# An attention and two-layer gated network kernel: the last matrix product of batches 2 and 3 in seven 16-bit products

## The chip, the cores and the metric

One core of one Trainium2 chip. The metric is the device time of one execution in microseconds; it is 1033.1 us as the median of 3 runs before the change (1030.32 to 1033.57). PE is TensorE, DVE VectorE, ACT ScalarE, POOL GpSimd, SP the engine whose queue issues the DMAs.

## What is computed

```python
local = softmax(causal(q @ k.T / 8)) @ v                   # 4 batches, 8 heads, 576 x 64
mem   = (phi(q) @ M_prev) / (phi(q) . z_prev + 1e-6)       # phi(x) = elu(x) + 1
x = g * mem + (1 - g) * local                              # (2304, 512) after the heads are joined
x = ((x @ w1) * (x @ w2)) @ w3 @ w_out                     # widths 1024, 1024, 512
y = (sigmoid(x @ w_gate) * (x @ w_val)) @ moe2_w_out       # width 1536, output (2304, 512)
```

All inputs are float32, and all products are made of two parts of each factor, high and low, of which three of the four combinations are added: three matmuls a product of blocks.

## The kernel before

The four batches of 576 tokens run one after the other. Tokens stand as columns, in two halves of 288 (`HS`), features as partitions in blocks of 128. At the start the weights are read as 64-bit bit patterns and turned to float32 (`conv_step`), `w3` and `w_out` are multiplied into one matrix, and the parts of the weights are stored in DRAM, from where they are loaded again for each batch.

Each batch passes through `ffn(b)` in four stages: **ab**, 8 column blocks of `(x@w1)*(x@w2)`; **xw**, 4 blocks of the product with the joined matrix, x2; **gv**, 12 blocks of gate times value, called hg; **ot**, 4 blocks d of the output from the 12 blocks of hg. Attention of the next batch is a generator whose steps `drive` lets in between, in proportion to the costs that `ffn` yields (`FRAC`, `ftot`); in gv none are let in. PE's order is the program's order; on the other engines a scheduler places the instructions.

In batches 0 and 1 all products are plain. In batches 2 and 3, ab and gv are computed by seven products instead of eight (Strassen's scheme in Winograd's form): the two column halves and the two row halves of the operand give x11, x12, x21, x22, sums of these are split into two float16 parts after a scale (`token_steps`, its steps `parts` and `sub`; a split is one ACT and one DVE instruction, `split_scaled`), and the weights have sums of their own. One weight unit of 8 blocks becomes part P (the blocks as they are) and part S (sums of them), each split to 16 bits. This is late work: `late_split` does one step at a time (P, the four sums, S), one step in `pace` calls of `pump`, reads from `kf` and stores to `ka` and `kb`. `two_rows` (line 509) runs the seven products of one column block, each of six matmuls (`prod2`, line 475) in a PSUM bank of its own out of three, and adds on DVE and POOL:

```python
        p1 = product(1, 1, 0, 0)
        s1 = tmp_("cy", "s1")
        nc.scalar.copy(s1, p1)
        p6 = product(6, 0, 0, 2)
        u2 = tmp_("cy", "u2")
        nc.vector.tensor_add(u2, p6, s1)
```

At its end it multiplies gate and value into `hraw` and splits that into two float32r parts, `hg` (`split_rows`, one ACT and one DVE or POOL instruction). The ot stage is plain in all four batches: 4 blocks x 2 halves x 12 blocks of hg x 3 matmuls = 288 (`prod`, line 467), an ACT copy to `osb` and one store for each block.

`pump` also loads weights ahead (`load_step`, line 382): five slots, in the last batch eight. `tails` (line 789) puts the steps that prepare x of batches 2 and 3 into `pending`, whose items run one by one among the ot products before.

## Time and profile before

| | |
|---|---|
| time, median of 3 runs | 1033.1 us |
| the profiled execution | 1028.78 us |
| its span, first to last instruction | 1026.8 us |
| mean granted TensorE clock | 0.993 |
| busy DVE, ACT, POOL | 684.5, 571.8, 247.4 us |
| DMA | 224.83 MB, mean 219 GB/s |

In the trace the stages begin at about these times: batch 0's gv at 263, ot at 345; batch 1's ab 385, xw 471, gv 504, ot 574; batch 2's ab 629, xw 698, gv 734, ot 796; batch 3's ab 855, xw 899, gv 923, ot 985. A wait is read from the bracket at the end of a timeline row: the idle time of the engine before it and what ended it. A product and its weight load are two rows, PE and PEld, and overlap. The granted clock is given as a share of 2.4 GHz. A group's mean is that of single instructions; where instructions run on, the timeline merges them, and their common length over their count is the time in which one gives way to the next.

### The profile page before, as it was taken

What the parts mean: (1) busy time and instruction counts of PE and PEld (TensorE: products, weight loads), DVE (VectorE), ACT (ScalarE), POOL (GpSimd) and SP (SyncE); (2) the same over time, 40 slices, a digit from 0 to 9 for tenths busy, and PEclk for the clock granted to TensorE, in tenths of its full rate; (3) what the DMA queues carried; (4) which work ended last, traced back from release to release, by engine and by line L of the source; (5) the groups of instructions that cost most, each with busy time, mean ns of one, the idle gap of its engine ahead of it and who ended that gap; (6) DMA issues with size and microseconds to landing.
All of it is one profiled execution on the core that took longest, in us unless ns stands there. A gap on an engine that the chain in (4) does not pass through costs nothing.

```text
span 1026.8 us, 19856 instructions
## 1 busy us (share of the span) xinstructions
PE 1000.1 (97%) x7382; PEld 834.0 (81%) x7382; DVE 684.5 (67%) x1596; ACT 571.8 (56%) x1179; POOL 247.4 (24%) x246
## 2 busy tenths in 40 slices
PE   7999999999999998999999999899999999999998
PEld 3556787888999898898977788677877888897798
DVE  6865888778776627765566659998877427837730
ACT  7977786567777635654455444455644433235420
POOL 3454021212000201321101012453244302403420
PEclk9989999999999999999999999999999999999999
DMA  8865799857776479863777588655755335545551
GB/s 294 249 214 197 260 345 314 307 193 262 243 248 223 159 252 372 293 201 99 266 245 243 207 282 311 187 182 162 226 179 187 112 112 190 196 150 162 186 193 56
DMA packets 80376, 224.83 MB, mean 219 GB/s; under 512 B 10520, under 2 KB 22936, under 8 KB 80280
## 3 DMA queue, kind: packets, MB, share of 16 engines
q1 hardware_dynamic: 80280, 223.57, 64.2%
q8 instruction: 58, 0.95, 0.4%
q14 instruction: 38, 0.31, 0.1%
HBM read 165.34 MB, written 58.20 MB: 218 GB/s over the span
## 4 chain that ended last, share of the span: by engine, by line
PE 76%; DVE 6%; ACT 2%; issue 1%; DMA 1%; POOL 0%; SPq 0%; DVEq 0%; ACTq 0%; POOLq 0%
PE gv L467 14%; PE ot L467 14%; PE gvp L478 12%; PE ab L467 9%; PE xw L467 9%; PE abp L478 6%; PE s L902 3%; PE t L963 3%; PE o L1031 3%; PE o L1016 1%; PE wps L467 1%; PE o L1024 1%; DMA wraw<-kf 1%; DVE p L907 1%; PE qt L1000 0%
## 5 line engine op out<-in xcount | busy, mean ns | idle before, releaser
L478 PEld LDWEIGHTS <-wslot 128*128 128x128 f16 x1680 | 163.0, 98 | 47.3 <-issue 5.9
L933 POOL TENSOR_SCALAR p<-p,sm,omg 116x116 f32<-116x116 f32 (+4 forms) x100 | 87.3, 877 | 325.4 <-DVE sm L931 187.2
L467 PE MATMUL ot<-hg,wslot 128*128 128x288 f32 x1152 | 165.7, 299 | 0.0
L467 PEld LDWEIGHTS ot<-hg,wslot 128*128 128x128 f32 x1152 | 154.5, 188 | 6.5 <-issue 5.5
L467 PE MATMUL gv<-x,wslot 128*128 128x288 f32 (+1 forms) x1152 | 147.5, 290 | 0.2 <-ACT gsb L134 0.2
L478 PE MATMUL gvp<-x,wslot 128*128 128x288 f16 x1008 | 124.3, 286 | 1.1 <-DVE x L177 1.1
L467 PE MATMUL ab<-x,wslot 128*128 128x288 f32 x768 | 121.0, 308 | 0.2 <-DVE wpart L597 0.2
L134 ACT ACTIVATE p<-p,sm 116x116 f32<-116x116 f32 (+4 forms) x160 | 92.9, 583 | 43.7 <-DVE sm L907 43.5
L467 PE MATMUL xw<-h,wslot 128*128 128x288 f32 x768 | 113.7, 300 | 2.4 <-ACT h L570 1.1
L467 PEld LDWEIGHTS ab<-x,wslot 128*128 128x128 f32 x768 | 107.2, 193 | 7.9 <-issue 5.0
L467 PEld LDWEIGHTS xw<-h,wslot 128*128 128x128 f32 x768 | 103.6, 188 | 7.4 <-issue 3.0
L907 DVE CUSTOM_DVE_ANT_0 p<-s,msk 116x116 f32<-116x116 f32 (+4 forms) x160 | 67.9, 454 | 36.1 <-PE s L902 35.5
L478 PE MATMUL abp<-x,wslot 128*128 128x288 f16 x672 | 87.4, 286 | 1.7 <-DVE c11ab L544 1.2
L572 DVE TENSOR_TENSOR wslot<-wraw,wslot 128x512 fp32r<-128x512 f32 x76 | 56.1, 740 | 40.3 <-ACT wslot L570 40.0
L467 PEld LDWEIGHTS gv<-x,wslot 128*128 128x128 f32 x576 | 76.4, 188 | 0.5 <-ACT gsb L134 0.5
L963 PE MATMUL t<-idf,p 116*116 116x116 f32 x480 | 67.6, 270 | 6.4 <-DVE p L933 3.9
L963 PEld LDWEIGHTS t<-idf,p 116*116 116x116 f32 x480 | 53.6, 137 | 20.7 <-issue 5.2
L467 PEld LDWEIGHTS <-wslot 128*128 128x128 f16 x576 | 56.3, 98 | 14.2
L353 ACT ACTIVATE cy<-r 128x512 f32<-128x512 f32 x76 | 51.3, 675 | 12.0 <-DVE wraw L362 2.4
L570 ACT CAST wslot<-wraw 128x512 fp32r<-128x512 f32 x76 | 47.0, 620 | 17.3 <-PE gv L467 7.4
L362 DVE SCALAR_TENSOR_TENSOR wraw<-cy,cr 128x512 int32<-128x512 int32 x76 | 54.0, 738 | 2.5 <-ACT cr L354 2.3
L981 ACT COPY pt<-t 116x696 f32<-116x696 f32 (+2 forms) x74 | 47.2, 647 | 9.5 <-PE t L963 9.2
(156 smaller groups left out, 1550.5 us busy)
## 6 DMA issues: line engine op xcount, KB each, us to landing
wslot<-k SPq DMA_DIRECT2D x76, 512.0 KB, 4.2
wslot<-ka SPq DMA_DIRECT2D x40, 512.0 KB, 4.0
k<-wslot SPq DMA_DIRECT2D x36, 512.0 KB, 3.7
wraw<-kf SPq DMA_DIRECT2D x32, 512.0 KB, 6.6
wslot<-kb SPq DMA_DIRECT2D x40, 384.0 KB, 3.9
r<-in_gv_dram SPq DMA_DIRECT2D x24, 512.0 KB, 5.2
kf<-wraw SPq DMA_DIRECT2D x20, 512.0 KB, 3.2
ka<-wS SPq DMA_DIRECT2D x20, 512.0 KB, 4.9
```

Source lines behind the costliest of these rows:

```text
L134: ins = nc.scalar.activation(**kw)
L353: nc.scalar.activation(out=y, in_=hi, func=AF.Prelu, scale=2.0**-112, alpha=2.0**32)
L362: nc.vector.scalar_tensor_tensor(z, y, 3, tmp["r"], ALU.logical_shift_left, ALU.bitwise_or)
L467: paced["pe"] = nc.tensor.matmul(ps, w[:, wi, blk, :], x[:, xi, cols : cols + n], start=first and part == 0, stop=last and part == 2,)
L478: paced["pe"] = nc.tensor.matmul(ps, w[:, wi, blk + k, :], x[:, xi, k, :], start=k == 0 and part == 0, stop=k == 1 and part == 2,)
L570: nc.scalar.copy(dst[:, 0], src)
L572: eng.tensor_sub(dst[:, 1], src, dst[:, 0].bitcast(F32))
L902: nc.tensor.matmul(os_[hh], q_[r, 0, i * T : (i + 1) * T], k_[r, 1, c0:c1], start=x == 0, stop=x == len(terms) - 1,)
L907: nc.vector.tensor_tensor_reduce(out=ps_[hh][:, c0:c1], in0=os_[hh], in1=msk[:, SP - w + c0 : SP - w + c1], scale=-0.125, scalar=3.0e38 if ...
L933: lower(SHARE_N).tensor_scalar(ps_[hh][:, :w], ps_[hh][:, :w], sm[:, 6 + hh : 7 + hh], omg[:T, 2 * p + hh : 2 * p + hh + 1], ALU.mult, ALU ...
L963: nc.tensor.transpose(tp[:T, c : c + T], src[hh][:, j * T : (j + 1) * T], idf[:T, :T])
L981: nc.scalar.copy(to, got)
```

## The change

The ot stage of batches 2 and 3 is computed by seven 16-bit products too (`out_rows`, new). The 12 blocks of hg are four blocks each in three groups g; each group is quartered and turned into seven operands by `token_steps`. For a pair of output blocks (dp, two of them) each product is a sum over the three groups: 18 matmuls. The first three products open the three PSUM banks; three others are added onto these banks after they have been read; the seventh has a bank of its own. The order on PE is products 0, 1, 2 on group 0, then on group 1, then on group 2, and then products 3 to 6, each over its three groups.

With it come
- six more late weight tasks for `o2` (P and S each, from `ko` into `op` and `os`, stored in pieces), between those of gv and of ab, and a scale for them (`o2_scale`), from maxima taken in batch 0;
- in gv of batches 2 and 3: the blocks are left whole as `hq`, four to a group, in the buffers of the late work; a group's steps go into `queue`, and `two_rows` takes two of them a column block (`flush(1)`); the rest run before `out_rows`. A scale of hg (`hg_scale`) comes from maxima of x2;
- `two_rows`: products 2, 7 and 3 are added onto the banks of products 1, 6 and 5 after these are read; one DVE and one POOL addition fewer, in ab one ACT copy more;
- x of batches 2 and 3: the three sums that need no scale are made ahead of it (`tails`);
- five weight slots in the last batch too; output stores by halves; `FRAC` by batch (0.89 in batch 2), other paces.

```diff
-PACE = (5, 4, 4, 14, 4)
+PACE = (4, 4, 3, 14, 8, 4)
...
+    tasks = [(u, "P") for u in jobs[:F2]] + [(("o", *x), "PS") for x in pairs_of]
+    NFIRST = len(tasks)
+    tasks += [(u, "PS") for u in jobs[F2:]]
+    NPARTS = len(tasks)
+    tasks += [(u, "S") for u in jobs[:F2]]
...
     def two_rows(...):
-        p2 = product(2, 1, 2, 5)
+        product(2, 1, 2, 5, a)
         c11 = tmp_("asb", "c11")
-        nc.vector.tensor_add(c11, p2, s1)
-        gate(c11)
-        p7 = product(7, 0, 6, 3)
+        if sigmoid:
+            act_fn(out=c11, in_=a, func=AF.Sigmoid, scale=by)
+        else:
+            nc.scalar.copy(c11, a)
+        product(7, 0, 6, 3, b)
         u3 = tmp_("cr", "u3")
-        nc.vector.tensor_add(u3, p7, u2)
-        p3 = product(3, 0, 2, 4)
+        nc.vector.tensor_add(u3, b, s1)
+        product(3, 0, 2, 4, c)
...
+    def out_rows(b, dp, x, by):
+        s = take(7)
+        banks = {}
+        def product(i, g, xo):
+            onto = {3: 0, 4: 2, 5: 1}.get(i, i)
+            if onto == i and g == 0:
+                banks[i] = ps_f.tile([128, 512], F32, tag="f", name=f"otp{b}_{dp}_{i}")[:, :HS]
+            w = slot(s + i)
+            for k in range(2):
+                for part, (wi, xi) in enumerate(((0, 0), (1, 0), (0, 1))):
+                    paced["pe"] = nc.tensor.matmul(
+                        banks[onto], w[:, wi, 2 * g + k, :], x[g][xo][:, xi, k, :],
...
+        for g in range(2):
+            for i, xo in ((0, 0), (1, 1), (2, 2)):
+                product(i, g, xo)
+        p1 = product(0, 2, 0)
+        nc.scalar.activation(out=s1, in_=p1, func=AF.Copy, scale=by[:, 0:1])
+        p5 = product(1, 2, 1)
+        nc.scalar.activation(out=s5, in_=p5, func=AF.Copy, scale=by[:, 0:1])
+        p6 = product(2, 2, 2)
+        plus(u2, p6, s1)
+        for i, xo in ((3, 5), (4, 3), (5, 4), (6, 6)):
+            for g in range(3):
+                ps = product(i, g, xo)
...
     gv of batches 2 and 3:
+                for _ in two_rows(take(2), x2, f"gv{b}_{f}", left, right, x2back[:, f : f + 1], True):
+                    pass
+                if f == 2:
+                    hgs, oback = hg_scale(b, x2top, x2s)
+                if f % 4 == 3:
+                    steps = token_steps(f"hg{b}_{g}", *quads, hg, lambda: hgs[:, 0:1], tags, tied=True)
+                    first = [steps[x] for x in ("p0", "t1", "p1", "t2", "p2")]
+                    then = [steps[x] for x in ("p5", "t3", "p3", "p4", "t4", "p6")]
+                    if g == 2:
+                        n = max(0, len(queue) - len(then))
+                        rest = [None] * (len(then) - len(queue[n:])) + queue[n:]
+                        queue[n:] = first
+                        for a, z in ((0, 1), (1, 3), (3, 4), (4, 6)):
+                            queue.extend(x for x in rest[a:z] + then[a:z] if x)
+                    else:
+                        queue.extend(first + then)
...
+        flush(len(queue))
+        for dp in range(2 if b > 1 else 0):
+            yield from out_rows(b, dp, hs, oback)
```

**DVE, end of batch 3's gv.** The names: `gvp_11` is the last block's products, `hraw` and `hq` its result, `hg` the split operands; `hq_8_0`, `hq_8_1`, `hq_10_0`, `hq_10_1` are the four quarters of the third group, and `hg_2_0`, `hg_2_2`, `hg_2_5`, `hg_2_6` hold its operands 0 and 1, 2 and 3, 5 and 4, 6. Before:

```order
L534 TENSOR_TENSOR u2gv_11_12487<-gvp_11_6_12480,s1gv_11_12478 128x288
L572 TENSOR_TENSOR hg_10_12391<-hgraw_10_12392,hg_10_12391 128x576
L544 TENSOR_TENSOR c11gv_11_12507<-gvp_11_2_12500,s1gv_11_12478 128x288
L549 TENSOR_TENSOR u3gv_11_12517<-gvp_11_7_12510,u2gv_11_12487 128x288
L553 TENSOR_TENSOR u4gv_11_12498<-gvp_11_3_12519,u4gv_11_12498 128x288
L559 TENSOR_TENSOR u3gv_11_12517<-u3gv_11_12517,gvp_11_4_12529 128x288
L525 SCALAR_TENSOR_TENSOR hgraw_11_12468<-s5gv_11_12496,x2back_11441,u4gv_11_12498 128x288
L525 SCALAR_TENSOR_TENSOR hgraw_11_12468<-u3gv_11_12517,x2back_11441,c11gv_11_12507 128x288
```

Here the last block ends DVE's work ahead of the output. After the change, from the last block's two multiplications on (three more steps of the second group stand between the last subtraction and these):

```order
L585 SCALAR_TENSOR_TENSOR hq_10_1_12395<-s5gv_11_12493,x2back_11494,u2gv_11_12483 128x288
L585 SCALAR_TENSOR_TENSOR hq_10_0_12394<-u3gv_11_12512,x2back_11494,c11gv_11_12504 128x288
L181 SCALAR_TENSOR_TENSOR hg_2_0_12535<-hq_8_0_12251,hgs_11890,hg_2_0_12535 128x576
L555 TENSOR_TENSOR hq_8_1_12252<-hq_10_1_12395,hq_8_1_12252 128x576
L181 SCALAR_TENSOR_TENSOR hg_1_6_12562<-hq_6_0_12108,hgs_11890,hg_1_6_12562 128x576
L181 SCALAR_TENSOR_TENSOR hg_2_5_12548<-hq_10_1_12395,hgs_11890,hg_2_5_12548 128x576
L555 TENSOR_TENSOR hq_8_0_12251<-hq_10_1_12395,hq_8_0_12251 128x576
L181 SCALAR_TENSOR_TENSOR hg_2_5_12548<-hq_10_0_12394,hgs_11890,hg_2_5_12548 128x576
L181 SCALAR_TENSOR_TENSOR hg_2_2_12542<-hq_8_1_12252,hgs_11890,hg_2_2_12542 128x576
L555 TENSOR_TENSOR hq_10_0_12394<-hq_8_0_12251,hq_10_0_12394 128x576
L181 SCALAR_TENSOR_TENSOR hg_2_2_12542<-hq_8_0_12251,hgs_11890,hg_2_2_12542 128x576
L181 SCALAR_TENSOR_TENSOR hg_2_6_12566<-hq_10_0_12394,hgs_11890,hg_2_6_12566 128x576
```

The row that writes `hg_2_2` from `hq_8_0` is operand 2, which product 2 on the third group reads; it stands eleventh here, behind operands 4, 5 and 3 of its group and operand 6 of the group before.

**ACT, the same place.** Before, the last gate, the cast of the last block, and the output copies:

```order
L134 ACTIVATE c11gv_11_12507<-c11gv_11_12507,x2back_11441 128x288
L134 ACTIVATE u4gv_11_12498<-u4gv_11_12498,x2back_11441 128x288
L570 CAST hg_11_12467<-hgraw_11_12468 128x576
L758 COPY osb_0_12543<-ot_0_0_12544 128x288
L758 COPY osb_0_12543<-ot_0_1_12584 128x288
```

After, the high parts of the operands, with the readings of the first two output products (`s1ot`, `s5ot`) between them:

```order
L180 ACTIVATE hg_2_0_12535<-hq_8_0_12251,hgs_11890 128x576
L180 ACTIVATE hg_1_6_12562<-hq_6_0_12108,hgs_11890 128x576
L180 ACTIVATE hg_2_5_12548<-hq_10_1_12395,hgs_11890 128x576
L180 ACTIVATE hg_2_5_12548<-hq_10_0_12394,hgs_11890 128x576
L668 ACTIVATE s1ot_0_12618<-otp_0_0_12569,hgs_11890 128x288
L180 ACTIVATE hg_2_2_12542<-hq_8_1_12252,hgs_11890 128x576
L671 ACTIVATE s5ot_0_12620<-otp_0_1_12578,hgs_11890 128x288
L180 ACTIVATE hg_2_2_12542<-hq_8_0_12251,hgs_11890 128x576
L180 ACTIVATE hg_2_6_12566<-hq_10_0_12394,hgs_11890 128x576
```

The high part of operand 2 stands behind `s5ot`, and so behind the eighth product on PE.

**DVE, ab of batch 1,** around its fifth column block (`hraw_4`). Before, with one late P split:

```order
L646 TENSOR_TENSOR hraw_4_5321<-ab_4_1_1_5432,asb_4_1_5430 128x288
L177 SCALAR_TENSOR_TENSOR wP_5473<-wraw_11_5213,wsc,wP_5473 128x1024
L172 TENSOR_REDUCE htop_4779<-hraw_4_5321 128x1
L907 ISA p_1_3_0_5447,sm_1_3_5449<-s_1_3_0_0_5450,msk 116x464
L907 ISA sm_1_3_5449 116x1
L907 ISA p_1_3_1_5448,sm_1_3_5449<-s_1_3_0_1_5451,msk 116x464
L907 ISA sm_1_3_5449 116x1
L572 TENSOR_TENSOR h_4_5320<-hraw_4_5321,h_4_5320 128x576
L646 TENSOR_TENSOR hraw_5_5465<-ab_5_0_1_5496,asb_5_0_5494 128x288
```

After, with a P split and the four sums of the first `o2` task (`wrawl`, `o2s`):

```order
L781 TENSOR_TENSOR hraw_4_5401<-ab_4_0_1_5451,asb_4_0_5449 128x288
L181 SCALAR_TENSOR_TENSOR wP_5488<-wrawl_5270,o2s,wP_5488 128x768
L1120 TENSOR_SCALAR sm_1_2_5457<-sm_1_2_5457 116x2
L428 TENSOR_TENSOR wrawl_5270<-wrawl_5270 128x256
L1121 RECIPROCAL sm_1_2_5457<-sm_1_2_5457 116x2
L429 TENSOR_TENSOR wrawl_5270<-wrawl_5270 128x256
L1123 TENSOR_SCALAR p_1_2_0_5455<-p_1_2_0_5455,sm_1_2_5457,omg 116x348
L430 TENSOR_TENSOR wrawl_5270<-wrawl_5270 128x256
L781 TENSOR_TENSOR hraw_4_5401<-ab_4_1_1_5515,asb_4_1_5513 128x288
L431 TENSOR_TENSOR wrawl_5270<-wrawl_5270 128x256
L176 TENSOR_REDUCE htop_4851<-hraw_4_5401 128x1
```

The sums stand between the attention steps (`sm`, `p`) and the multiplications that read PSUM.

## Rows read from the trace of the kernel before

**Rows 1.** page, busy time of each engine and its share of the span.
```profile
PE 1000.1 (97%) x7382; PEld 834.0 (81%) x7382; DVE 684.5 (67%) x1596; ACT 571.8 (56%) x1179; POOL 247.4 (24%) x246
```

**Rows 2.** windows: stretch, length, busy us (instructions) of PE, PEld, DVE, ACT, POOL; clock, DMA.
```profile
392.00:471.00 79.00, 76.56 (x581) 66.67 (x580) 57.73 (x144) 43.98 (x99) 22.95 (x19) 0.98 0.73 255
471.00:504.00 33.00, 33.00 (x258) 31.19 (x257) 16.89 (x56) 14.90 (x36) 8.79 (x7) 1.00 0.50 167
629.00:655.00 26.00, 24.12 (x193) 17.44 (x191) 24.61 (x65) 14.15 (x35) 11.78 (x13) 1.00 0.80 273
655.00:698.00 43.00, 41.38 (x333) 30.64 (x332) 39.57 (x105) 20.03 (x47) 21.66 (x22) 1.00 0.53 170
734.00:796.00 62.00, 61.68 (x504) 49.04 (x502) 44.81 (x94) 31.41 (x61) 25.82 (x28) 1.00 0.58 191
796.00:855.00 59.00, 59.00 (x455) 51.19 (x453) 25.38 (x77) 26.43 (x55) 11.47 (x10) 1.00 0.37 119
923.00:985.00 62.00, 61.71 (x505) 49.19 (x503) 44.60 (x93) 32.22 (x62) 25.45 (x28) 1.00 0.55 182
985.00:1023.30 38.30, 38.24 (x289) 38.01 (x287) 1.34 (x3) 4.03 (x10) 1.47 (x2) 1.00 0.32 106
```

**Rows 3.** waits of PE: who waited for whom, us in total, times, longest.
```profile
PE gvp L478 <- DVE x L177: 1.1, 3, 0.4
```

**Rows 4.** chain of waits, batch 3: start, length, engine, tile, line, instructions.
```profile
927.84 57.24 PE gvp L478 x466
985.09 38.17 PE ot L467 x288
```

**Rows 5.** timeline, end of batch 3's gate/value stage: start, length, engine, instruction.
```profile
984.83 7.40 PE L467 MATMUL ot<-hg,wslot 128*128 128x288 f32 x54
...
985.19 0.45 DVE L559 TENSOR_TENSOR u3gv<-u3gv,gvp 128x288 f32<-128x288 f32 x1 [0.28 <-PE gvp L478]
985.58 0.52 DVE L525 SCALAR_TENSOR_TENSOR hgraw<-s5gv,x2back,u4gv 128x288 f32<-128x288 f32 x1
986.01 0.51 DVE L525 SCALAR_TENSOR_TENSOR hgraw<-u3gv,x2back,c11gv 128x288 f32<-128x288 f32 x1
```

**Rows 6.** timeline, split steps of batch 3's x2, merged where they run on.
```profile
920.19 1.43 DVE L500 TENSOR_TENSOR x2f<-x2f,x2f 128x576 f32<-128x576 f32 x2 [7.14 <-ACT x2f L692]
...
921.53 2.27 DVE L177 SCALAR_TENSOR_TENSOR x<-x2f,x2s,x 128x576 f16<-128x576 f32 x3
```

**Rows 7.** timeline of PE, attention between output products of batch 2.
```profile
807.75 0.36 PE L902 MATMUL s<-qkh 64*116 64x232 f32 x2
...
808.26 0.67 PE L467 MATMUL ot<-hg,wslot 128*128 128x288 f32 x3
...
809.47 1.19 PE L1016 MATMUL o<-qts,ms 64*64 64x232 f32 x8
...
812.48 0.66 PE L467 MATMUL ot<-hg,wslot 128*128 128x288 f32 x3
813.07 1.38 PE L1031 MATMUL o<-pt,vs 116*64 116x344 f32 x12
```

**Rows 8.** timeline of PE, start of batch 1, and one window behind it.
```profile
397.61 0.58 PE L963 MATMUL t<-idf,p 116*116 116x116 f32 x4 [2.44 <-DVE mn L849]
397.96 5.36 PE L467 MATMUL ab<-x,wslot 128*128 128x288 f32 x27
...
400.00:402.00 2.00, 2.00 (x10) 2.00 (x10) 2.00 (x3) 0.78 (x2) 0.00 (x0) 0.50 1.03 416
```

**Rows 9.** groups by line, VectorE: count, busy us, mean ns of one, idle before.
```profile
L177 DVE SCALAR_TENSOR_TENSOR wS<-wraw,wsc,wS 128x1024 f16<-128x1024 f32 x20 | 26.0, 1300 | 5.9 <-ACT wS L176 5.7
...
L177 DVE SCALAR_TENSOR_TENSOR x<-x2f,x2s,x 128x576 f16<-128x576 f32 x14 | 11.1, 818 | 4.7 <-ACT x L176 4.7
...
L177 DVE SCALAR_TENSOR_TENSOR wP<-wraw,wsc,wP 128x768 f16<-128x768 f32 x8 | 8.1, 1010 | 0.3 <-ACT wP L176 0.3
```

**Rows 10.** timeline, the last copy of the kernel.
```profile
1023.28 0.40 ACT L758 COPY osb<-ot 128x288 f32<-128x288 f32 x1 [4.35 <-PE ot L467]
```

More of the change, by code (lines that the diff above doesn't have):

```diff
@@ L248, in tile_attention_memory_ffn, with flush @@
     done = []
+    queue = []
+    def flush(n):
+        while queue and n > 0:
+            queue.pop(0)()
+            n -= 1
     def in_use(tag):
@@ L479, in prod2, with token_steps @@
                     ps, w[:, wi, blk + k, :], x[:, xi, k, :],
-                    start=k == 0 and part == 0, stop=k == 1 and part == 2,
+                    start=not more and k == 0 and part == 0, stop=k == 1 and part == 2,
+                    skip_group_check=more,
                 )
-    def token_steps(name, x01, x23, ops, scale):
+    def token_steps(name, b11, b12, b21, b22, ops, scale, tags, apart=False, tied=False):
         both = {}
-        b11, b12 = x01[:, :, :HS], x01[:, :, HS:]
-        b21, b22 = x23[:, :, :HS], x23[:, :, HS:]
+        t = {1: b11, 2: b11, 3: b12, 4: b21}
         def parts(m, src):
@@ L509, in two_rows, with sub, step @@
-    def two_rows(s, x, name, ht, hraw, by, sigmoid, cost=0.0):
+                    both[m // 2] = fp.tile([128, 2, 2, 2, HS], F16, tag=tags[m // 2], name=f"{name}_{m}", bufs=1)
+                o = both[m // 2][:, m % 2]
+                for ins in split_scaled(o[:, 0], o[:, 1], src(), scale()):
+                    if tied:
+                        behind(ins)
+                ops[m] = o
+            return step
+        def sub(n, a, b):
+            def step():
+                if apart and n < 3:
+                    t[n] = fp.tile([128, 2, HS], F32, tag="hraw", name=f"{name}_t{n}")
+                ins = nc.vector.tensor_sub(t[n], a(), b())
+                if tied:
+                    behind(ins)
+            return step
@@ L517, in product @@
             pump()
             return ps
[L520 to L522 removed]
         def times(out, a, b):
             nc.vector.scalar_tensor_tensor(out, a, by, b, ALU.mult, ALU.mult)
[L527 removed]
+        a = product(1, 1, 0, 0)
         yield cost
         s1 = tmp_("cy", "s1")
[L530 to L531 removed]
+        nc.scalar.copy(s1, a)
+        b = product(6, 0, 0, 2)
@@ L552, in two_rows @@
         release(s)
-        nc.vector.tensor_add(u4, p3, u4)
+        nc.vector.tensor_add(u2, c, u2)
         nc.gpsimd.tensor_add(s5, u3, s5)
-        gate(u4)
+        if sigmoid:
+            act_fn(out=u2, in_=u2, func=AF.Sigmoid, scale=by)
         p4 = product(4, 1, 4, 6)
```

300 lines of the change are left out of this document (204 added, 96 removed).

## The prediction

> **What bounds the kernel now.** I read the page's busy shares first: PE is at 97% of the span [rows 1], so the question is which PE time goes and which new wait comes. The windows by stage come next [rows 2]: PE is full from the first product of batch 1 on, and VectorE has room in some stages and none in others. In the first 26 us of batch 2 VectorE is busy 24.61 us and PE idles 1.9; in the gate/value stages of batches 2 and 3 (734:796, 923:985) VectorE is busy 44.8 and 44.6 of 62 and PE loses about 0.3. The list of waits confirms the latter: PE waited there 1.1 us in all on the splits of x2 [rows 3]. The chain of waits gives the two cadences on which the gain rests: 466 16-bit products in 57.24 us, 0.1228 us each, and 288 output products in 38.17 us, 0.1325 us each [rows 4]. Both are 128x288, both run on without gaps.
>
> **Term 1, the product itself.** Per batch the old output product is 288 matmuls, the new one 2 column-block pairs x 7 products x 18 = 252. Old 288 x 0.1325 = 38.2; new 252 x 0.1228 = 30.9. That is -7.2 us for batch 3, where nothing else is on PE, and the same for batch 2, whose attention matmuls only move: **-14.4 us**. Here a rule speaks against the row. The Trainium skill, "TensorE: Matmul & The Clock Gate", section "Back-to-back issue gap", gives the isolated gap by columns alone; by it both kinds would take an estimated 122.5 ns, only the 36 matmuls fewer would count, 4.4 us a batch, and the sum below would come out 5.6 us worse. The trace agrees with it for the 16-bit products and not for the old ones, at 132.5; the measurement decides.
>
> **Term 2, the handover into batch 3's output product.** Before, each column block of the gate/value stage was split when it was done, and the first output product began with blocks long ready: PE ran on while VectorE subtracted the last block (PE starts at 984.83, the last results follow to 986.5) [rows 5]. Now the third group of four blocks can be turned into its seven operands only when its last block is done, and PE comes to its third operand as ninth product. How late is that operand? Time 0 is PE's first output matmul.
> - VectorE reads a product 0.36 us after its end (985.19 against 984.83) [rows 5]. The second product of the last block ends 5 x 6 x 0.1228 = 3.7 before 0, so VectorE takes it up at -3.3. From there to the last block's final subtraction the order has three splits, two sums and three additions. Back to back, three splits took 2.27 and two sums 1.43 [rows 6]; a PSUM addition gives way after 0.39 (985.19 to 985.58). Together 4.9 us, and some 0.5 of waits for PE and ScalarE: the subtraction ends near 2.5, where it ended near 0.8 before.
> - The bank it reads is the one that the third output product opens. That would start at 1.5 and starts at 2.6: **1.2 us**.
> - After the subtraction VectorE has, ahead of the split that the ninth product needs, 7 more splits, 4 sums and 2 multiplications: 8 x 0.757 + 4 x 0.715 + 2 x 0.43 = 9.8 us (0.43 is 985.58 to 986.01) [rows 5, 6]. It is done at 12.4. PE without any wait would be there after 8 products, 8 x 6 x 0.1228 = 5.9. So PE loses **6.5 us** in all, the 1.2 included, some 5 of them in one piece. Bounds: 4.7, if VectorE reaches the subtraction without backlog (0.4 + 0.4 + 9.8 = 10.6), and 8, if each sum-to-split step also waits for ScalarE. Behind the waiting product stand 33 more on PE; nothing else can go ahead.
>
> **Term 3, the same in batch 2.** Between the first nine products stand attention groups: an s group of 0.5 (807.75 to 808.26), a t group of about as much, the o groups of 3.0 (809.47 to 812.48) and 1.4 [rows 7]. PE arrives at 5.9 + 5.4 + 1.2 = 12.5. VectorE's row also holds eight attention instructions, at the 0.33 us of that window's mean (25.38 us over 77) [rows 2] 2.6 us: ready at 15.0. PE loses 1.2 + 2.5 = **3.7 us**; bounds 1.5 and 6.
>
> **Term 4, the clock after a wait.** In batch 1 PE waited 2.44 us (397.61), and the granted clock then stood at the lower level, 1.2 GHz (0.50 of full), at 400 to 402; 27 matmuls that took 0.1325 each elsewhere, 3.6 in all, took 5.36 [rows 8]. A wait of that size therefore cost 1.8 more. Here part of the slow stretch will fall into the longer wait itself: I take 1.0 for each of the two, **+2**; bounds 0 and 3.6.
>
> **Term 5, VectorE in the gate/value stages.** Each block loses one addition (five to four) and its ordinary split; each group brings 7 splits and 4 sums, each batch four maxima of x2. Counted by block with the length of single instructions (addition 0.45, multiplication 0.52 [rows 5], split 0.82 [rows 9], sum 0.72 [rows 6]), a block after the first has 3.1 to 5.3 us of vector work against the 42 x 0.1228 = 5.16 us of its products; the first block of batch 2 has 7.3, since a late weight task lies in it. The banks allow two products, 1.5 us, of delay. I take **+1**; bounds 0 and 8 (a rival below).
>
> **Term 6, six more late weight tasks in batch 1.** One is a 6-block split, four sums and an 8-block split: 1.01 + 4 x 0.45 + 1.30 = 4.1 us on VectorE [rows 5, 9] (a sum of 256 columns is priced as the addition of 288), 25 us for six, at one step in four pumps through the a/b stage and into the next (392 to 504). VectorE is busy 57.7 + 16.9 of these 112 us [rows 2]; it becomes 89%. Where it was at 95 and 92% (629:655, 655:698) PE lost 1.9 of 26 and 1.6 of 43 us. By these some 3 us would be lost here, of which 2.4 are there already: **+1**; bounds -4 (the gap of rows 8 with its slow clock goes) and +4. Their loads and stores are one queue's, SP's; the weights of this stage are fetched five slots ahead, and that hides them.
>
> **Term 7, the a/b products of batches 2 and 3.** Three of seven products add onto a bank that was read; the order of products leaves the same two products between a read and the next write, so PE loses nothing by it. VectorE has one addition fewer per block, GpSimd too, and two late tasks fewer lie in batch 2; attention comes denser. Of the 3.5 us that PE idles from 629 to 698 I take **-2** (bounds 0 and -3.5).
>
> **No cost:** the x sums ahead of the scale (VectorE only, under a full PE), the scale of hg (its small matmul stands a whole block behind the maxima it sums), halves of maxima in batch 0, the ring of five slots in batch 3 (batch 2 ran with five). Cover gone, each is a wait of one VectorE step, under 1 us. The last store is half as large: **-0.3** of the 3.5 us that follow the last copy [rows 10].
>
> **Sum:** -14.4 + 6.5 + 3.7 + 2 + 1 + 1 - 2 - 0.3 = -2.5 us. The profiled execution took 1028.8, so it would be 1026.3; the runs' median is 1033.1, 0.4% above it, and against that I forecast **1030.6**. A measurement of this kernel can tell about 0.3%, 3.1 us, from no change.
>
> **The rivals.**
> - *The handover is short.* VectorE without backlog (4.7), batch 2's attention as cover (1.5), no slow clock, and batch 1's gap gone: -14.4 + 4.7 + 1.5 + 0 + 1 - 2 - 2 - 0.3, about -11, or -7 with one of them missing: 1022 to 1026, say 1024. For it: PE is in order but the clock did not fall in any wait under 1 us. Against: the order puts 9.8 us behind the last subtraction, whatever comes before. Chance 0.25.
> - *VectorE and ScalarE become the bound of the gate/value stages.* Place: the eight blocks of each batch that carry one or two split steps. Each step is ScalarE's half, then VectorE's; if a VectorE instruction waits there for ScalarE with the next addition behind it, the bank is late. Price: 0.5 us for each of 16 blocks, 8 us, so 5 to 6 us slower: 1039. It decides from the point where a block takes more than 5.16 us. For it: three blocks have 5.2 to 5.3 of vector work. Against: ScalarE was at 32 of 62 us. Chance 0.2.
> - *The new product is no faster per matmul*, because 132.5 belonged to the stage and not to the number format: 504 x 0.0097 = 4.9 dearer, 1035.5. Against it: the s-free stretches of both formats [rows 4]. Chance 0.05. The Trainium skill's gap rule, named above, gives nearly this result by a different road, both kinds at one price.
> - The forecast, half of the gain eaten and a bit more, has 0.5; its own range is 1026 to 1035.
>
> **Numbers.** The range 1022 to 1040 takes in the short handover and the late engines, and leaves out some 0.15. Faster by over 0.3%: all of the first rival and a third of the forecast, 0.42. Within: 0.36. Slower: the second rival, half of the third, some of the forecast, 0.22.
>
> **What would show it.** In the profile after: output products at 0.123 us; a wait of 4 to 6 us of PE for VectorE (or for the split) in front of the ninth output product of batch 3 and one of 2 to 4 in batch 2, with a granted clock below 1 behind them; gate/value stages of still 62 us. Wrong, if those stages take 66, if no wait over 2 us stands at the handover, or if the time moves in batch 0.

## The result and the profile after

The changed kernel takes 1037.6 us as the median of 20 runs, the kernel before 1032.6 of 20: a ratio of 1.0051 (95% interval 1.0037 to 1.0065). It is 0.5% slower, where 0.2% faster was forecast. The profiled execution took 1036.7 us, its span is 1034.9.

The two spans differ by 8.1 us, the medians by 4.9: the profiled execution of the kernel before is the fastest of its 20, 3.8 us under its median, that of the changed kernel is 0.9 under its own. In the table (its last three kernels are experiments below) a stage lasts from its first matmul to the next stage's first matmul, by PE's timeline; the last one ends with the last instruction of a compute engine. The stretch up to batch 1's a/b stage changes from one profile to the next (two profiles of the kernel before differ there by 7.8 us), the later stages of that kernel hardly. The granted clock is one reason: batch 0's output stage took 53.4 us in the second profile, at a mean of 0.94, and 50.5 in the first, at 1.00. So causes are read from the stages behind batch 1's a/b stage: there the change costs 8.4 us, and the a/b stage gives 1.2 to 2.6 back.

| stage | before | before, second profile | changed | no hg steps (e11) | part alone (e7) | mended (f5) |
|---|---|---|---|---|---|---|
| up to batch 1's a/b | 385.9 | 393.7 | 388.8 | 388.6 | 391.9 | 390.0 |
| batch 1, a/b | 85.1 | 83.7 | 82.5 | 81.7 | 83.5 | 84.0 |
| batch 1, the other three | 158.0 | 157.9 | 159.2 | 159.2 | 157.9 | 158.3 |
| batch 2, a/b | 62.3 | 62.4 | 62.4 | 62.4 | 60.7 | 63.3 |
| batch 2, x2 | 40.7 | 40.8 | 45.2 | 45.2 | 40.7 | 45.2 |
| batch 2, gate/value | 62.7 | 62.8 | **67.5** | 65.7 | 63.8 | 65.9 |
| batch 2, output | 60.2 | 60.2 | **54.1** | 48.2 | 60.2 | 51.1 |
| batch 3, a/b and x2 | 67.7 | 67.7 | 67.9 | 67.5 | 67.7 | 67.5 |
| batch 3, gate/value | 62.1 | 62.1 | **65.3** | 63.8 | 63.2 | 63.9 |
| batch 3, output | 38.9 | 38.9 | **39.4** | 31.7 | 38.9 | 33.2 |

The windows of the changed kernel at the x2, gate/value and output stages, with the columns of [rows 2]:

```profile
692.90:738.10 45.20, 43.32 (x333) 37.08 (x331) 30.85 (x94) 26.37 (x59) 14.10 (x11) 1.00 0.33 109
738.10:805.60 67.50, 63.13 (x508) 49.30 (x507) 53.27 (x110) 33.58 (x66) 9.99 (x12) 1.00 0.54 176
805.60:859.70 54.10, 49.58 (x392) 34.78 (x390) 33.01 (x78) 25.67 (x49) 9.04 (x9) 0.97 0.45 126
927.60:992.90 65.30, 62.78 (x507) 49.29 (x507) 49.70 (x104) 32.15 (x64) 9.46 (x12) 1.00 0.50 166
992.90:1031.80 38.90, 33.84 (x253) 25.53 (x251) 16.14 (x27) 9.42 (x16) 2.21 (x3) 0.91 0.47 139
```

Where PE lost 1.1 us in both gate/value stages together [rows 3] (the window of [rows 2] begins behind batch 2's first wait), it now idles 4.4 and 2.5; VectorE has gone from 45 to 53 and 50 us of work, GpSimd from 26 to 10. In the output stages PE idles 4.5 and 5.1 us, and the granted clock is below 1. The list of PE's waits names the causes (`gvp` and `otp` are the gate/value and output products in PSUM, `u2` and `u3` additions of VectorE that read them, `bcol` the column that the total of x, `xsum`, is made from):

```profile
PE otp L638 <- DVE hg L181: 3.9, 2, 2.4
PE otp L638 <- ACT hg L180: 3.5, 2, 2.7
PE gvp L527 <- DVE x L181: 3.4, 5, 1.1
PE gvp L527 <- DVE u2gv L594: 3.4, 8, 0.9
PE otp L638 <- DVE u3gv L622: 1.5, 2, 0.7
PE xsum L172 <- DVE bcol L979: 1.4, 2, 0.8
```

The three `otp` rows are the handovers from the gate/value to the output stage, 8.9 us; before there was no such wait. The two `gvp` rows are the gate/value stages: [rows 3] had 1.1 us for x and nothing for u2. A wait costs more than its idle time, since the last product ahead of it runs out alone: a single product takes 0.286 us (the mean in the page's row below), in a row one gives way to the next after 0.123. By these two numbers I estimate 0.16 us more for each wait.

```profile
L527 PE MATMUL gvp<-x,wslot 128*128 128x288 f16 x1008 | 126.2, 286 | 6.9 <-DVE x L181 3.4
```

**The handover of batch 3** in the timeline (PE, VectorE and one row of ScalarE; the first output matmul starts at 992.86):

```profile
994.73 0.44 DVE L622 TENSOR_TENSOR u3gv<-u3gv,gvp 128x288 f32<-128x288 f32 x1
...
995.23 4.57 PE L638 MATMUL otp<-hg,wslot 128*128 128x288 f16 x36 [0.74 <-DVE u3gv L622]
...
997.65 0.51 DVE L585 SCALAR_TENSOR_TENSOR hq<-u3gv,x2back,c11gv 128x288 f32<-128x288 f32 x1
998.08 0.81 DVE L181 SCALAR_TENSOR_TENSOR hg<-hq,hgs,hg 128x576 f16<-128x576 f32 x1
...
1001.61 1.54 DVE L181 SCALAR_TENSOR_TENSOR hg<-hq,hgs,hg 128x576 f16<-128x576 f32 x2
1001.72 0.77 ACT L180 ACTIVATE hg<-hq,hgs 128x576 f16<-128x576 f32 x1 [0.83 <-DVE hq L555]
1002.54 0.64 PE L638 MATMUL otp<-hg,wslot 128*128 128x288 f16 x2 [2.75 <-ACT hg L180]
...
1003.73 0.81 DVE L181 SCALAR_TENSOR_TENSOR hg<-hq,hgs,hg 128x576 f16<-128x576 f32 x1
...
1004.59 1.84 PE L638 MATMUL otp<-hg,wslot 128*128 128x288 f16 x7 [1.41 <-DVE hg L181]
```

Operand 2 of the third group has its high part at 1002.5 and its low part at 1004.5. That is 11.7 us after the first output matmul; 12.4 was worked out. The clock fell with the wait, as three windows of 2 us show (columns of [rows 2]): 1.00 in its first part, 0.50 when PE goes on.

```profile
1000.00:1002.00 2.00, 0.00 (x0) 0.00 (x0) 2.00 (x4) 1.17 (x3) 0.00 (x0) 1.00 0.91 281
...
1004.00:1006.00 2.00, 1.41 (x7) 0.87 (x7) 1.61 (x3) 0.68 (x1) 0.00 (x0) 0.50 0.00 0
1006.00:1008.00 2.00, 2.00 (x10) 1.29 (x9) 0.27 (x1) 0.00 (x0) 0.00 (x0) 0.50 0.58 166
```

**The start of batch 3's gate/value stage** on ScalarE, the changed kernel:

```profile
930.03 0.40 ACT L599 COPY s5gv<-gvp 128x288 f32<-128x288 f32 x1 [0.78 <-PE gvp L527]
930.45 1.28 ACT L137 ACT_TABLE_LOAD   x1
931.74 0.50 ACT L137 ACTIVATE c11gv<-gvp,x2back 128x288 f32<-128x288 f32 x1
932.14 0.76 ACT L180 ACTIVATE x<-x2f,x2s 128x576 f16<-128x576 f32 x1
```

and the kernel before, at the same place:

```profile
925.19 0.40 ACT L538 COPY s5gv<-gvp 128x288 f32<-128x288 f32 x1 [0.78 <-PE gvp L478]
926.04 0.78 ACT L176 ACTIVATE x<-x2f,x2s 128x576 f16<-128x576 f32 x1 [0.45 <-DVE x2f L500]
926.83 1.28 ACT L134 ACT_TABLE_LOAD   x1
```

Before, the last high part of x2 came ahead of the sigmoid's table load, now behind it: the gate reads its bank of PSUM directly, so it is ready earlier than the last sum of x2, and the scheduler put it first (e7 below, with the accumulation alone, has the same order). The prediction looked at this place only for VectorE. The Trainium skill, "ScalarE: Activation LUTs", section "What ACT_TABLE_LOAD costs", gives about 1283 ns for the load and some 1380 ns of drain with every switch; the load agrees (1.28), a drain does not show: the sigmoid starts 0.01 us behind the load, the load 0.02 behind the copy.

### The profile page after: what moved, and what is told of

Its sections match the earlier page's. It is cut to its first block, busy times and chain, and to the rows that moved or that the text cites. A ratio compares the mean times of both kernels' runs of the same rounds, so it can differ in the third digit from the quotient of the medians.

```text
span 1034.9 us, 19915 instructions
## 1 busy us (share of the span) xinstructions
PE 992.5 (96%) x7314; PEld 806.1 (78%) x7314; DVE 746.8 (72%) x1714; ACT 598.4 (58%) x1221; POOL 206.4 (20%) x201
## 4 chain that ended last, share of the span: by engine, by line
PE 65%; DVE 13%; ACT 3%; DMA 3%; issue 2%; POOL 0%; SPq 0%; DVEq 0%; ACTq 0%; POOLq 0%
PE gv L516 14%; PE gvp L527 9%; PE xw L516 9%; PE ab L516 8%; PE ot L516 6%; PE abp L527 5%; PE otp L638 5%; PE s L1092 3%; PE t L1153 3%; PE o L1221 3%; DVE hg L181 2%; PE o L1206 1%; DVE p L1097 1%; DMA wrawl<-kf 1%; PE o L1214 1%
## 5 line engine op out<-in xcount | busy, mean ns | idle before, releaser
L527 PEld LDWEIGHTS <-wslot 128*128 128x128 f16 x1680 | 162.7, 98 | 56.2 <-issue 15.3
L1123 POOL TENSOR_SCALAR p<-p,sm,omg 116x116 f32<-116x116 f32 (+4 forms) x100 | 91.0, 915 | 326.6 <-DVE sm L1121 213.2
L516 PE MATMUL ab<-x,wslot 128*128 128x288 f32 x768 | 118.2, 302 | 0.5 <-ACT asb L778 0.3
L516 PEld LDWEIGHTS ab<-x,wslot 128*128 128x128 f32 x768 | 104.2, 188 | 8.4 <-issue 5.3
L516 PE MATMUL ot<-hg,wslot 128*128 128x288 f32 x576 | 83.5, 299 | 0.0
L516 PEld LDWEIGHTS ot<-hg,wslot 128*128 128x128 f32 x576 | 77.3, 188 | 4.7 <-issue 3.2
L638 PE MATMUL otp<-hg,wslot 128*128 128x288 f16 x504 | 69.5, 295 | 8.8 <-DVE hg L181 3.9
L1153 PE MATMUL t<-idf,p 116*116 116x116 f32 x480 | 67.7, 270 | 5.7 <-DVE p L1123 4.8
L638 PEld LDWEIGHTS <-wslot 128*128 128x128 f16 x504 | 49.9, 101 | 25.7 <-issue 12.0
L516 PEld LDWEIGHTS <-wslot 128*128 128x128 f16 x576 | 56.3, 98 | 14.2
```

The lines of the kernel that those rows point to most:

```text
L516: paced["pe"] = nc.tensor.matmul(ps, w[:, wi, blk, :], x[:, xi, cols : cols + n], start=first and part == 0, stop=last and part == 2,)
L527: paced["pe"] = nc.tensor.matmul(ps, w[:, wi, blk + k, :], x[:, xi, k, :], start=not more and k == 0 and part == 0, stop=k == 1 and part == 2,
L638: paced["pe"] = nc.tensor.matmul(banks[onto], w[:, wi, 2 * g + k, :], x[g][xo][:, xi, k, :], start=onto == i and g == 0 and k == 0 and par ...
L1123: lower(SHARE_N).tensor_scalar(ps_[hh][:, :w], ps_[hh][:, :w], sm[:, 6 + hh : 7 + hh], omg[:T, 2 * p + hh : 2 * p + hh + 1], ALU.mult, ALU ...
L1153: nc.tensor.transpose(tp[:T, c : c + T], src[hh][:, j * T : (j + 1) * T], idf[:T, :T])
```

## The experiments

Two theories at the start: the loss is the handover with its slow clock (A), or it is the gate/value stages (B). All times are medians; the kernel before, measured beside each, took 1032.1 to 1032.4.

**Without the steps of hg.** In `token_steps` of hg:

```diff
+                if tied:
+                    behind(nc.gpsimd.memset(o.bitcast(F32), 0.0078))
+                    ops[m] = o
+                    return
```

(e1; in e2 the condition is `tied and name.endswith("_2")`, the third group alone; e11 with the memsets queued over the blocks instead of at the end.)

> Leaves out all splits and sums of hg in batches 2 and 3 (the operands are filled with a constant by GpSimd), so nothing on VectorE or ScalarE makes an output product wait. Theory: the time was lost to these steps, 7.9 us in the two gate/value stages (67.5 and 65.3 us against 62.8 and 62.1 before), 3.9 and 4.9 us of waits at the two handovers and some 5 us of lower clock behind them. All of it goes: gate/value stages 62 to 63.5, no wait over 0.5 us in front of an output product, full clock: about 1018 us. Rival: the stages are long because the new gate/value product itself (accumulation onto read banks, the maxima of x2) is slower; then they stay at 65 to 67 and the time is about 1025.

> Leaves out the splits and sums of the third group of hg alone. Theory: the handover waits come from the third group, and the lower clock from the waits; the gate/value stages stay as long as in the changed kernel (within 1 us) because groups 0 and 1 are split inside them. Waits 8.8 us and clock 5 us go: about 1025 us. Rival: PE then waits for the steps of the second group that are left over at the same place, two thirds of the waits stay: about 1033 us.

> As the first run (all splits and sums of hg in batches 2 and 3 left out), but the filling by GpSimd is spread over the column blocks, since its 6.3 us in one piece delayed GpSimd's addition of the last block and so the third output product (2.23 and 0.88 us). Theory: those 3 us go too: 1021, which is what the product would take if splitting hg were free. Rival: the third bank is late for another reason: 1024.

e1 took 1024.3, e2 1030.1 (between its two cases), e11 1019.4 us (ratio to before 0.990, 0.986 to 0.993). The memsets in one piece had themselves cost 5 us in e1, and e2 shares that fault (2.87 and 1.46 us of wait for `u3gv`), so its number only bounds the third group's price from below. In e11 the chain ends with one row:

```profile
982.50 30.88 PE otp L644 x252
```

252 products in 30.88 us, 0.1225 each: term 1 to the digit (30.9). So the steps of hg cost 18.1 us by the medians (with some 4 to either side), more than the product saves; the table has 13.6 of it in the output stages (5.9 and 7.7), 3.2 in the gate/value stages. Theory A holds for most of it. But the gate/value stages stay 3.0 and 1.7 us longer than before with no step of hg in them: the first run's rival was half right.

**The order at the handover.** e5 puts every step that is let in after operand 2 of the third group behind it (`after2` orders an instruction behind the one kept, on its queue, without a semaphore):

```diff
+                        after2(ins)
+                if tied and m == 2 and name.endswith("_2"):
+                    paced["p2"] = ins
```

e9n lets the steps in by need: operands 5 of both groups behind operand 2, then, between the output products, 3, 4 and 6:

```diff
-                        queue[n:] = first
-                        for a, z in ((0, 1), (1, 3), (3, 4), (4, 6)):
-                            queue.extend(x for x in rest[a:z] + then[a:z] if x)
+                        rest = queue[-len(then):]
+                        queue[-len(then):] = first + [rest[0], then[0], rest[1], then[1]]
+                        held[:] = [[rest[2], then[2]], [rest[3], then[3], rest[4], then[4]], [rest[5], then[5]]]
...
         plus(u2, p6, s1)
+        more()
```

> Nothing is left out; on VectorE and ScalarE all steps that are let in after operand 2 of the third group now stand behind it (they stood ahead: operands 3, 4, 5 of the group and the leftover steps of the second group). Theory: the handover waits are a matter of this order: operand 2 is ready some 4.7 us after the first output product instead of 11.7, the waits of 2.75 and 1.41 us before the ninth product of batch 3 and of 0.73 and 2.44 in batch 2 go, smaller ones of 1 to 3 us in all come at later products, and the lower clock behind the wait goes: about 1032 us (of 1037.5). Rival: VectorE has the same work to do and PE waits as long, at products 11 to 13: 1037.

> The changed kernel with the order of need alone: 1031.9 (e5) less the 3.3 and some 1.5 us for the third bank: about 1027. If the waits come back at operand 3 or 4 instead: 1031.

e5 took 1031.9 us, its first case, though with 5.8 us of later waits where 1 to 3 were expected; e9n took 1029.5, between its two cases. The work on every engine is the same. Batch 3's output went from 39.4 to 34.6 and 33.2 us, and its clock stays at 1.00; batch 2's went only from 54.1 to 53.4 and 53.1. PE's waits at output products, in e5:

```profile
PE otp L651 <- DVE u2ot L667: 4.1, 2, 3.3
...
PE otp L651 <- ACT s1ot L681: 1.4, 1, 1.4
```

and in e9n:

```profile
PE otp L639 <- DVE u3gv L623: 1.5, 2, 0.7
...
PE otp L639 <- DVE hg L181: 0.4, 1, 0.4
```

So batch 3's waits of 2.75 and 1.41 us were a matter of order, not of the amount of work. In batch 2 e9n only moved the wait (there were 0.73 and 2.44): VectorE's attention step came late, and PE waited for it, with the clock down again behind it (a row of the timeline, and a window).

```profile
828.32 0.78 PE L1160 MATMUL t<-idf,p 116*116 116x116 f32 x6 [2.27 <-DVE p L1130]
```

```profile
830.00:832.00 2.00, 2.00 (x11) 1.64 (x10) 0.41 (x1) 0.00 (x0) 0.09 (x1) 0.50 0.58 94
```

There VectorE's load counts as well: in e9 below, with most sums on GpSimd, one of 0.97 stands in place of this wait, the clock stays at 1.00, and the stage takes 49.4 us.

**VectorE's load.** e4 gives the sums of two groups to GpSimd:

```diff
+                eng = nc.gpsimd if tied and not name.endswith("_2") else nc.vector
-                ins = nc.vector.tensor_sub(t[n], a(), b())
+                ins = eng.tensor_sub(t[n], a(), b())
```

> The eight sums of the first two groups of hg go from VectorE (0.74 us each) to GpSimd (about 1.4 us each, by the low parts of h there), in each batch. Theory: the gate/value stages are long because VectorE is late with the additions that free PSUM banks: 5.9 us of VectorE a batch less, the waits for u2gv (3.4 us in all) mostly go and the backlog at the handover shrinks by a step or two: about 1034 us. Rival: GpSimd's longer sums and their two handovers delay the chain of steps and slow VectorE: 1038 to 1040.

1034.8 us. The 2.8 us came as expected (2.6 by the stages; by the medians the ratios to before, 1.0034 and 1.0051, have intervals that overlap), but from elsewhere: the output stages went to 52.5 and 37.0, the gate/value stages to 68.1 and 66.2, longer than without the edit. In batch 3's output stage PE waits as long as in the changed kernel (4.8 us in all against 4.9). What was saved there is the clock, which stays at 1.00 in this execution, though one of the waits is 2.51 us (window of the stage, columns of [rows 2]):

```profile
992.20:1029.10 36.90, 31.50 (x254) 24.53 (x251) 16.95 (x26) 8.88 (x15) 3.92 (x4) 1.00 0.50 146
```

A sum takes 1.49 us on GpSimd and 0.75 on VectorE; the waits for `u2gv` rose from 3.4 to 4.7 us. Less load on VectorE did not shorten these stages; since GpSimd's sums came later, the run doesn't tell what the load costs there. e11 does: 3.2 us for all steps of hg.

**The start of the gate/value stages.** The part alone on the kernel before (e7) is the new `two_rows` with its old end; e3 lets the maxima in from the second block on, e6 adds a sigmoid of two numbers; f1 is e11 with both.

```diff
-        if b > 1:
+                if f == 1:
             for n, m in enumerate((0, 1, 5, 4)):
...
+            if b > 1 and d == KC - 1:
+                t = fp.tile([128, 4], F32, tag="early", name=f"early{b}", bufs=1)
+                act_fn(out=t[:, :2], in_=x2s, func=AF.Sigmoid)
```

> The kernel before with one part of the change alone: in the seven products of the a/b and gate/value stages, products 2, 7 and 3 are added onto read banks in PSUM. Theory: the table load comes ahead of the last split of x2 here too, with a wait of about 1 us in each of batches 2 and 3, and the a/b stages gain little: gate/value stages of 64 us each, a/b as before: 1034 to 1035 against 1032.6 of the kernel before. Rival: one addition a block fewer on VectorE and on GpSimd relieves the a/b stage of batch 2 (3 us of idle PE): 1031.

> The four maxima of x2 come one column block later, behind the last splits of x2 on VectorE. Theory: in the changed kernel they stand ahead of the split that the third product of the first block needs (waits of 0.56 and 0.87 us in batch 3, 0.45, 1.15, 0.39 and 0.93 in batch 2): some 2.5 us of the 7.9 go, about 1035 us, and the stages become 65.5 and 64.2. Rival: VectorE is full there and the maxima cost the same one block later: no difference, 1037.5.

> A sigmoid of two numbers at the last x2 block of batches 2 and 3 brings the 1.28 us table load of ScalarE forward. Theory: in the changed kernel the first gate reads its PSUM bank directly, so the table load and the gate stand ahead of the high part of the last x2 operands on ScalarE, where before they stood behind it: 1.4 us in batch 3 and some 2.5 in batch 2 of the longer gate/value stages. They go: stages of 64 and 65 us, time about 1034. Rival: the maxima of x2 on VectorE keep the split late anyway: at most 1 us, 1036.5 to 1037.5.

> As the run with no hg steps (spread filling; the output product then reads a constant), with the sigmoid table early and the maxima of x2 a block later as well. Theory: the two together hold the start of the gate/value stages, each hidden by the other: batch 3's stage falls from 63.8 to 62.3 us (62.1 before the change), batch 2's from 65.8 to about 64 (the late weight sums stay): 1019.4 less 3, about 1016.5. Rival: the accumulation onto read banks is what lengthens the stages: no change, 1019.4.

e7: 1034.0 us (ratio 1.0019, 0.9996 to 1.0042, so not shown to differ from the kernel before), gate/value stages 63.8 and 63.2, a/b of batch 2 60.7: by the stages the accumulation gains 1.6 us there and loses 2.2 here, to a wait that the kernel before did not have:

```profile
PE gvp L478 <- ACT x L176: 1.6, 2, 0.8
```

e3 (1037.4) and e6 (1038.1) changed nothing that the time shows (batch 3's stage fell by 0.4 and 0.7): with the maxima gone the split waits for ScalarE, with the table load gone for VectorE. f1, with both, took 1018.1, not shown to differ from e11's 1019.4; its stages are what tells: 62.3 in batch 3 (62.1 before the change), 65.2 in batch 2. There two waits of about 0.95 are left, for an addition that stands on VectorE among the late weight sums (`wrawl`) and the maxima (VectorE's timeline, and the row of PE's waits):

```profile
743.80 0.74 DVE L176 TENSOR_REDUCE x2top<-x 128x2 f32<-128x576 f16 x1
744.46 0.41 DVE L430 TENSOR_TENSOR wrawl<-wrawl 128x256 f32<-128x256 f32 x1
744.79 0.45 DVE L600 TENSOR_TENSOR u2gv<-gvp,s1gv 128x288 f32<-128x288 f32 x1
```

```profile
PE gvp L527 <- DVE u2gv L600: 1.9, 2, 1.0
```

In f5 below, which lets no weight step into the first three blocks of this stage, both waits are gone.

**The pace of the weight work in batch 2.** The diff changes `PACE[4]` from 4 to 8; f4 sets it back.

```diff
-PACE = (4, 4, 3, 14, 8, 4)
+PACE = (4, 4, 3, 14, 4, 4)
```

> The changed kernel with the pace of late weight work in batch 2's second half at 4 instead of 8, as in the kernel before: one task's sums and split come out of the first blocks of batch 2's gate/value stage. Theory: the waits of 0.93 for u2gv and part of the 1.15 and 0.45 us for x in that stage go, 67.5 to 66 us: 1036. Rival: they wait for ScalarE and the maxima, and the work only moves to the x2 stage: 1037.5.

1039.3 us: the gate/value stage fell by 1.9 to 65.5, but x2 rose by 2.9 to 48.1, by a wait of 2.01 us for ScalarE's part of the softmax (`p`) with the clock at 0.52 in the window 704 to 706 behind it. So the weight sums were the last part of batch 2's loss there. By the stages the pace of 4 is 1 us dearer than the change's 8; the medians (1039.3 of 10 runs, 1037.6 of 20) don't tell the two apart.

**The total of x.** e10 puts `finish_x` one place later in `pending`:

```diff
-            first, run("t1", "t2", "t3"), lambda: finish_x(b, mx),
+            first, run("t1", "t2", "t3"), lambda: None, lambda: finish_x(b, mx),
```

> The changed kernel with the total of x put one place later in PE's order. Theory: the sums made ahead of the scale stand on VectorE in front of the total's column, and PE waits 0.76 and 0.62 us for it: 1.4 us go, 1036.2. Rival: the later scale makes x late for the a/b product, and the a/b stages lose as much: 1037.5.

1037.8 us, the rival's number. Its mechanism is not shown, though: batch 1's and batch 2's output stages lost their waits of 0.76 and 0.62 (54.8 and 53.4 us), and the new wait of 0.84 in batch 3's a/b stage gives back only 0.4 of this; the stages up to there gained 1.1, which is less than the medians can tell.

**Together.** e8 is e4, e5 and e6; e9 is e9n, e3, e6, e10 and more sums on GpSimd; f2 is e9n, e3, e6, f4, e10 in batch 1 alone and GpSimd's sums in batch 2 alone; f3 is f2 without GpSimd's sums; f5 is f2 with the pace of 8, and no weight step in the first three blocks:

```diff
+                if b == 2 and f in (0, 3):
+                    ws["pace"] = (0, 8)[f // 3]
```

> The changed kernel with three mends at once: sums of groups 0 and 1 on GpSimd, operand 2 of the third group first, the table load early. If the three causes are separate, what they give adds up: 2.8 (measured for the sums alone) + 5 + 3, about 1027 us. If they overlap (the sums help only the same handover waits that the order removes): about 1029.

> The whole product with every cause that the traces showed mended: VectorE's steps at the handover in the order in which PE needs their operands (5 of groups 2 and 3 right behind operand 2 of the third, then the reading of the third bank, then 3, 4, 6), the sums on GpSimd except the two that lead to operand 2 of the third group, the sigmoid table early and the maxima of x2 a block later, the total of x one place later. Theory: e5's 1031.9 less 3.3 us of waits for the third bank in batch 2, some 1.5 of 2.2 in batch 3, 2 to 3 at the starts of the gate/value stages (the two mends there hid each other when done alone) and 1.4 for the total of x: about 1024 us, clearly faster than both kernels. Rival: GpSimd's longer sums put the same waits back, as in e8: 1030 to 1033.

> The changed kernel with the order of need, the sigmoid table early, the maxima later, the pace of 4, the total of x later in batch 1 alone, and the sums of groups 1 and 2 of hg on GpSimd in batch 2 alone (there they gave 49.4 against 53.1 us for the output stage, in batch 3 they cost 2 us). Theory: 1029.5 (order of need alone) less 3.7 (batch 2's output), 1.5 and 0.7 (starts of the gate/value stages), 0.7 (total of x): about 1023 to 1025. Rival: the mends share their gains, 1028.

> The same without GpSimd's sums. If the sums in batch 2 are worth the 3.7 us that its output stage showed: 1027 to 1028, 3 above the last. If the slow clock behind a wait made that difference, and the other mends remove the wait too: equal to it.

> As f2 (all mends, sums on GpSimd in batch 2), but the pace is the change's own 8 again, and no late weight step is let into the first three blocks of batch 2's gate/value stage, where the maxima lie. Theory: the x2 stage of batch 2 is 45.2 us again (48.0 in f2), the gate/value stage 64 to 65: 1028.2 less 2.5, about 1025.5. Rival: the steps kept back come in where the hg steps are and put 2 us back there: 1028.

Measured: 1032.8, 1029.1, 1028.2, 1028.6 and 1026.8 us; against the kernel before, f5 stands at 0.9945 (0.9923 to 0.9967). It beats both kernels, by medians the changed one by 10.8 us. e8 gave less than even its second case, f2 came out with its rival and e9 near it: f2's pace of 4 put its x2 stage at 48.0. f3 came out with its second case, f5 between its two. f2 and f3 don't differ by more than the runs scatter (in batch 2, f2's sums save 2.0 us in the output stage and cost 0.9 in the gate/value stage), so GpSimd's sums are not shown to be worth anything in the time once the order is right. Nor is f5 shown to be faster than f2 or f3. In f5 PE's waits at output products are those of e9n (1.4 and 0.4), and batch 2's x2 stage is 45.2 again; the gate/value stages keep 3.2 and 1.8 us of their loss.

**The kernel before, once more.**

> The kernel before, unchanged, for a second profile. Theory: the stages from batch 1's gate/value stage on repeat within 0.3 us, the first 120 us and the a/b stage of batch 1 (low clock at 409 in the first profile) differ by up to 4 us: so only the sum of the stages tells what the change costs. Rival: the start repeats too (117.6), and the 2.8 us there belong to the change.

One execution, 1035.1 us. From batch 1's x2 stage on no stage differs by more than 0.1 us from the first profile; up to there the two differ by 6.3. So the start doesn't repeat (120.3 us, the changed kernel's is 120.4), and the 2.8 us there don't belong to the change. The differences reach further than expected: 2.8 in the start, -1.4 in batch 1's a/b stage, but also 1.3 and 2.9 in batch 0's x2 and output stages. The first profile's low clock in batch 1 is at 399 to 402 [rows 8], not at 409. The windows of the second profile for batch 2's output and batch 3's gate/value and output stages:

```profile
801.20:861.40 60.20, 60.20 (x465) 52.05 (x462) 26.26 (x79) 26.97 (x56) 11.69 (x11) 1.00 0.37 118
929.10:991.20 62.10, 61.81 (x506) 49.24 (x505) 44.76 (x93) 32.32 (x62) 25.29 (x28) 1.00 0.55 184
991.20:1030.10 38.90, 38.44 (x291) 38.20 (x288) 1.44 (x4) 4.41 (x10) 1.67 (x2) 1.00 0.32 104
```

## Why the prediction was wrong

The time lies in the range, the direction does not. One of its own signs of being wrong came: the gate/value stages took 67.5 and 65.3 us. By its steps:

- **Term 1, -14.4:** right. 0.1225 us a product in e11, and batch 3's output stage there is 38.9 - 31.7 = 7.2 shorter. The Trainium skill's gap rule ("TensorE: Matmul & The Clock Gate", section "Back-to-back issue gap") gives an estimated 122.5 ns for these, and the run agrees; the old products' 132.5 [rows 4], which it does not give, were a real part of the gain.
- **Terms 2 and 3, +6.5 and +3.7:** the mechanism was right at its place, 4.9 (0.74 + 2.75 + 1.41) and 3.9 (0.74 + 0.73 + 2.44) measured, 5.4 and 4.4 with an estimated 0.16 for each wait. That their sum of 9.8 meets the 10.2 is partly luck, one being less and one more than forecast. e9n shows for batch 3 that the order was the cause; in batch 2 the order alone gave 1.0 us.
- **Term 4, +2:** too small, an estimated 3.8 (2.3 and 1.5). PE is busy 33.84 us in batch 3's output stage against 31.07 in e11, and 49.58 in batch 2's against 47.58 (windows of the same stages): 2.8 and 2.0 more for the same products, of which the three waits explain an estimated 0.5 each. The clock stayed down over 7 us in batch 3 (1002 to 1009), not only for some 3 us around the window of [rows 8]. Neither size is fixed: five profiles with nearly these waits (the changed kernel, e3, e6, e10, f4) have 38.5 to 39.9 us for that stage, and the wait of [rows 8] itself was not followed by a low clock in the second profile (last section).
- **Term 5, +1, is the step that failed:** 4.7 + 3.2 = 7.9 us (67.47 - 62.74 and 65.29 - 62.11). "A block after the first has 3.1 to 5.3 us of vector work against the 42 x 0.1228 = 5.16 us of its products" counted VectorE, block by block. The steps of hg cost 3.2 there (e11). Nearly 5 us came from the start of each stage (its first 18 us in batch 2, its first 7 in batch 3), for which the prediction counted a full first block in batch 2 but no wait: 2.0 from the order of ScalarE's table load and VectorE's maxima (f1 against e11: 0.56 and 1.45), 2.4 in batch 2 from the late weight sums (f4 gives 1.9 of it back, and f5 is without these waits), 0.2 unexplained. The accumulation, costed at nothing because "the order of products leaves the same two products between a read and the next write", was cheap for PE's banks and moved a queue on another engine.
- **Term 6, +1:** a gain of 0.9 to 2.3 (a/b -2.6 or -1.2 by the profile of before that is taken, x2 +0.4).
- **Term 7, -2:** about -1. e7 has 1.6 in the a/b stage. In the change, attention is denser in the a/b and x2 stages (`FRAC`), so only the three stages together tell: without the gate/value stage batch 2 gained 1.5, of which -7.2 + 4.4 + 1.5 + 0.8 (product, handover, clock, the wait for the total of x) make -0.5.
- **No cost** for the sums of x: PE waited 1.4 us for the total behind them (0.76 in batch 1's output stage, 0.62 in batch 2's), 1.7 with the run-out, an entry that should have had a row.
- **The last store, -0.3:** 0.5. The span ends 2.6 us behind the last instruction of a compute engine, where it was 3.1.

Of the rivals, the late engines (1039, chance 0.2) came nearest in time. Their price of 8 us in the gate/value stages was met by 7.9, but their mechanism, a step pair that fills a block, is at most 3.2 of it: that the sizes agree is luck. Put together, from batch 1's x2 stage on (worked out before rounding): 1.2 for batch 1, -1.5 for batch 2 without its gate/value stage, 7.9 for the two gate/value stages, 0.2 and 0.6 for the rest of batch 3, 8.4. By the terms, -14.4 + 9.8 + 3.8 + 7.9 + 0.4 - 1 + 1.7 is 8.2, of which the -1 was itself worked out as a remainder. Batch 1's a/b stage and the last store take part of that back; the rest of the way to the 4.9 of the medians lies in what one or two profiles can't tell, the stretch up to batch 1 above all, and stays open.

## What to carry to other kernels

When an engine is given work in front of a consumer, read the order of its queue as well as its load: with the same work, the order of need took 8 us off this kernel (7.2 by its two output stages, 6.2 of them in batch 3). An edit that lets one instruction become ready earlier can move it ahead of others on its own engine; look there for a table load and for whom it delays. Where two causes stand at one place, take them away together: here each alone measured as nothing (e3, e6).
